# Later weight loads, a ring of queries beside 40 P places, and early gelu products in an attention and gMLP kernel

## The chip, the cores and the metric

The kernel runs on one core of a Trainium2 chip. A core has five engines with queues of their own: TensorE (PE in the profile, with its weight loads as PEld), VectorE (DVE), ScalarE (ACT), GpSimd (POOL) and SyncE (SP), which here only issues DMAs. The metric is device time in microseconds for one execution, as the median of several runs. A profile is one execution of its own, so its time stands beside that median and is not the same number.

## What is computed

Two rounds of an attention layer A and a gated MLP layer B on one sequence of 2048 rows of 512 values, each with a residual addition. A is multi-query attention: 32 heads of 16 values share one key and one value head.

```python
def _A_ref(x, wq, wk, wv, wo):
    ...
    q = (lambda x, *d: x.transpose(*d))((x @ wq).reshape(B, S, H, Dh), 0, 2, 1, 3)
    k = x @ wk
    v = x @ wv
    scores = jnp.einsum('bhqd,bkd->bhqk', q, k) * Dh ** (-0.5)
    p = _softmax(scores, axis=-1)
    o = jnp.einsum('bhqk,bkd->bhqd', p, v)
    return (lambda x, *d: x.transpose(*d))(o, 0, 2, 1, 3).reshape(B, S, H * Dh) @ wo

def _B_ref(x, w_in, w_sp, b_sp, w_out):
    ...
    z = _gelu(jnp.einsum('bsd,df->bsf', x, w_in))
    z1 = z[..., :Fh].copy()
    z2 = _layernorm(z[..., Fh:], axis=-1)
    g = jnp.einsum('ts,bsf->btf', w_sp, z2) + b_sp[None, :, None]
    return jnp.einsum('bsf,fd->bsd', z1 * g, w_out)
x = A_x
x = x + _A_ref(_layernorm(x, axis=-1), A_wq, A_wk, A_wv, A_wo)
x = x + _B_ref(_layernorm(x, axis=-1), B_w_in, B_w_sp, B_b_sp, B_w_out)
```

The last two lines are done twice with the same weights. All values are bfloat16.

## The kernel before

**Scores and P.** A layer has 2048 score blocks of 128 keys by 512 query columns. Up to four blocks are one pack of matmuls (L1262), one block in each of four PSUM banks. Most blocks are turned into P by ScalarE (`do_exp`, L1470), one bank at a time or two neighbouring banks in one instruction. The others go to VectorE as a sum of three clipped linear terms: the first term is read from PSUM (L1384, here a block "on DVE"), the two others are made from it by GpSimd or VectorE, one or two blocks at a time (L1389). A finished P block of 128 x 512 takes one of `NPS` places in the tensor `Pb`; a block on DVE takes three. The product with V (PV, L1525) empties the places again.

**Queries and keys.** `attn_inputs` goes over the 16 tiles of 128 rows: layer norm, a transpose to xnT (the first two tiles by TensorE, the others by a DMA issued on SP, L539), keys and values (L753 to L773), queries (L783, put to `Q` by L793). While not all keys are there, two units run side by side over the keys as they come (the ramp); then the units follow one another. Query rows fall into eight chunks, of 128, 128, 256, 512, 512, 256, 128 and 128 rows.

**The MLP inside the attention.** When a chunk is done it is normalised, multiplied by wo (L942), and its part of layer B begins. `mlp_in` makes one batch for a group of chunks: the products with w_in for z2 (L998, 448 columns at a time) and for z1 (L1044), each ended by a gelu on ScalarE (L1003, L1058). Since exp and gelu need different tables on ScalarE, a batch stops new score packs, loads the gelu table (L1712), runs all its gelus and goes back. There are five batches in a layer: four inside the attention and a last one behind it. The spatial product with w_sp (L1105, `spatial`) is filled in between score packs; its last pass (`last_pass`) runs at the end of a layer: matmuls L1141, the gate product with z1, the product with w_out (L1170) and the addition to X (L1174). In layer 0 the partial sum `gp` is added on TensorE (identity matmul L1139) and the gate product is made by VectorE (L1149). In layer 1 VectorE adds (L1149) and GpSimd multiplies (L1160); `NOID` says which.

**What sets the order.** The order of the instructions on each engine is worked out while the program is built: `Sched` keeps a free time for every engine, every task has an estimated duration, a priority and sometimes a gate (a condition that must hold), and at each step the ready task of the best priority is taken. Smaller numbers come first. On the chip each engine follows this fixed order and waits on semaphores. On PE, packs come first, then PV, then other products that fit before the next pack is due (`pack_due`, `SLACK`); `keep_warm` (L1644) puts in products with zeros where PE would be mostly idle. `SHARE` is the share of blocks for VectorE. SP is one queue too: all loads and all DMA transposes stand in it one behind the other. `setup` puts the loads there:

```python
        for a in range(4, NT, 4):
            loadx(a, a + 4)
        self.ldo = self.dma(self.wo[:], ..., 524288, prio=1)
        self.ldin = self.dma(self.w_in[:], ..., 1835008, prio=1)
        self.ldout = self.dma(self.w_out[:], ..., 917504, prio=1)
```

They are followed there by a load of `bspc`, the bias row of the spatial product, and by the transposes of xn.

Of the kernel before, what the change touches and what calls it, by code (L numbers as in the profile page):

```python
# [12 lines left out]
P = 128  # L13
# [6 lines left out]
S = 2048  # L20
# [272 lines left out]
class Attn:  # L293

    def __init__(self, K, layer):
        self.K = K
        self.layer = layer
        self.kdep, self.vdep, self.qdep = {}, {}, {}
        self.nxt = 0
        self.started = False  # L300
        self.full = False
        self.ugs = []
        for ci, (q0, nq) in enumerate(CHUNKS):
            ng = 512 // nq
# [11 lines left out]
        self.end = None  # L316
        self.chunk_ugs = {}
        for u in self.ugs:
            self.chunk_ugs.setdefault(u.ci, []).append(u)
# [69 lines left out]
class Kernel:  # L389

    SCORE_CAP = 6
    WSP_FROM = 25000
    NPS = 32
    PV_FREE = 6
# [6 lines left out]
    HOLD = 200  # L401
    POOL_ON = 3500
    A_ADJ = 1
    CAP_LINE = 8000
# [7 lines left out]
    NROT = (2, 2)  # L412
    SHARE = 0.31
    SHARE_HI = 0.34
# [8 lines left out]
    RAMP_SHARE1 = 0.0  # L423
    ACT_LOW = 1200
    POOL_MAX = 1400
# [5 lines left out]
    PV_LEAST = 6  # L431
    SLACK = 300
    SLACK_HI = 500
    MISC_T = 1500
    MISC_T2 = 1000
# [5 lines left out]
    def __init__(self, nc, es, ins, out):  # L441
        (self.A_x, self.A_wq, self.A_wk, self.A_wv, self.A_wo, self.B_x, self.B_w_in, self.B_w_sp, self.B_b_sp,
         self.B_w_out) = ins
        self.out = out
        self.nc = nc
        self.es = es
        self.s = Sched(nc)
        self.banks = Pool_(self.s, 8)
        self.score_held = 0
        self.misc_held = 0  # L450
        self.batches = []
        self.batch = None
        self.table = "exp"
# [13 lines left out]
    def alloc(self):  # L467
# [17 lines left out]
        self.w_out = self.sb([P, NF, D], BF16, "w_out")  # L485
        self.Q = self.sb([P, 4, S], BF16, "Q")
        self.xnT2 = self.sb([P, 1, KD, 512], BF16, "xnT2")
# [68 lines left out]
    def job(self, prio, pieces, consumers, tag, kind="misc", batch=None, spare=0, only=None):  # L556
# [4 lines left out]
        def gate():  # L561
            if only is not None and not only():
                return False
            av = self.banks.avail()
            if len(av) < 1 + spare:
                return False
            if kind == "z":
                return self.batch is batch
            if isinstance(kind, int) and self.ai <= kind:
                return False  # L570
            return self.misc_held < self.misc_cap()

        def hook(task):
            b = max(self.banks.avail(), key=lambda b: b.i)
            self.banks.take([b], task)
            hold["b"] = b
            if kind != "z":
                self.misc_held += 1

        last = None  # L580
# [102 lines left out]
    def setup(self):  # L683
# [17 lines left out]
        for a in range(4, NT, 4):  # L701
            loadx(a, a + 4)
        self.ldo = self.dma(self.wo[:], self.A_wo.rearrange("(c p) n -> p c n", p=P), 524288, prio=1)
        self.ldin = self.dma(self.w_in[:], self.B_w_in.rearrange("(kd p) f -> p kd f", p=P), 1835008, prio=1)
        self.ldout = self.dma(self.w_out[:], self.B_w_out.rearrange("(c p) n -> p c n", p=P), 917504, prio=1)
        self.ldv = ldv
# [70 lines left out]

    def queries(self, t, dep, war, prio):
        def qf(e, b, lo, hi):
# [7 lines left out]
        def mk(last, bank):  # L787
            o = self.Q[:, :, t * P:(t + 1) * P]

            def src():  # L790
                return self.ps32[:, bank(), :].rearrange("p (g c) -> p g c", g=4)
            return Task(None, None, None, [last] + list(war), prio - 0.5, tag="qev",
                        alts={"dve": (c_ps(512), lambda e: e.tensor_scalar(o, src(), QSCALE, None, op0=ALU.mult)),  # L793
                              "act": (c_act(512), lambda e: e.activation(o, src(), ACTF.Copy, scale=QSCALE))})
        def later():

            return self.ai < len(self.attns) and self.attns[self.ai].full
        made, outs = self.job(prio, [(lambda e, b: qf(e, b, 0, 2), c_mm(8, 128), [dep, self.ldq]),
# [3 lines left out]
    def attn_inputs(self, layer, xdeps):  # L802
# [5 lines left out]
        for t in range(NT):  # L808
# [8 lines left out]
            A.vdep[t] = [vout]  # L817
            m, q = self.queries(t, ev, war, pr + 0.01 if t < 2 else 4 + 0.05 * t)
            A.qdep[t] = q
# [263 lines left out]
    def spatial(self, B, pi, final):  # L1083
# [5 lines left out]
        for tc in range(4):  # L1089
# [37 lines left out]
    def last_pass(self, B, t, s0, n, sl, lds, zd, final, use):  # L1127

        tc, o = t // 4, (t % 4) * P
        noid = self.NOID[B.layer]  # L1130
        w = n if noid else n + 1
        hs = []
        for f0, f1 in ((0, 4), (4, NF)):
            def gf(e, b, lo, hi, f0=f0):
                ins = None
# [9 lines left out]

            def mk(lp, bank, f0=f0, f1=f1):
                def fn(e):
# [8 lines left out]
            B.all += made  # L1156
            if noid:
                def pf(e, f0=f0, f1=f1):
# [64 lines left out]
    def issue_pack(self, A, blks, deps, bs):  # L1223
        s = self.s
        k = len(blks)

        x = (self.RAMP_SHARE, self.RAMP_SHARE1)[A.layer] if not A.full else self.SHARE if self.pe_line() > self.PE_LINE else self.SHARE_HI
        self.credit = min(self.credit + k * x, self.CREDIT) if x else 0.0
        late = sum(1 for u, kt, j in blks if kt >= self.KT_ACT)
# [28 lines left out]
        def fn(e):  # L1258
            ins = None
            for i, (u, kt, j) in enumerate(blks):  # L1260
                q = self.Q[32 * j:32 * j + 32, u.g0:u.g0 + u.ng, u.q0:u.q0 + u.nq]
                ins = e.matmul(self.ps32[:, jb[i].i, :], self.kT[32 * j:32 * j + 32, u.half, kt * P:(kt + 1) * P], q,  # L1262
                               tile_position=(32 * j, 0), start=True, stop=True)
            return ins
# [515 lines left out]
    def check_batch(self):  # L1780
        if self.batch is None and self.batches:
            b = self.batches[0]
            if all(d.start is not None and d.done <= self.s.t for d in b.pre):
                self.batches.pop(0)
                b.pe_done = False
                self.batch = b
                return True
# [107 lines left out]
```

## Time and profile before

| | |
|---|---|
| median of 3 runs | 1602.91 us (1599.86 to 1607.8) |
| the profiled execution | 1609.46 us, its span 1607.7 us |
| granted TensorE clock over the span | 0.984 of full speed |
| exps (L1470) | 1934 instructions, 1343.4 us busy |
| first terms of blocks on DVE (L1384) | 1278, 835.6 us busy |
| other terms on POOL (L1389) | 1082, 908.7 us busy |
| other terms on DVE (L1389) | 499, 194.1 us busy |
| score matmuls (L1262), PV (L1525) | 4096 and 6652 |
| warm-up products (L1644) | 196 |

A busy time is the time in which an engine had at least one instruction under way; a row's mean is the length of one instruction, and neighbours overlap, so the sum of means can be above the busy time. The number behind a second bar in a row is the idle time of the engine just ahead of these instructions, and behind an arrow stands who ended it. PE's ends are modelled. The granted clock is the share of full speed that TensorE was given. In a timeline a row is a run of like instructions: start, length, engine, line, what it writes and reads, how many.

### The profile page before, as it was taken

The page shows a single profiled execution, that of the slowest core. Times are in us where ns is not written, and L with a number is a line of the kernel's source. Part 1 is how long each engine was busy: PE and PEld are TensorE (multiplying, and loading weights), DVE is VectorE, ACT ScalarE, POOL GpSimd, SP SyncE. Part 2 cuts the span into 40 slices and gives each one's busy share as a digit, 9 for nine tenths or more (in the row PEclk, how much of TensorE's full clock was granted, in tenths as well). Part 3 has the DMA queues.
Part 4 walks back from the last instruction along what each step waited for, and adds up shares of the span by engine and source line. Part 5 has one row for each costly group of instructions (what it writes and reads, how often), then busy time and mean ns, then how long its engine had stood idle before and what let it go on. Part 6 is the DMA issues. An engine that isn't in the chain of part 4 may idle for free.

```text
span 1607.7 us, 36520 instructions
## 1 busy us (share of the span) xinstructions
PE 1499.4 (93%) x14064; PEld 501.0 (31%) x14064; DVE 1389.6 (86%) x2625; ACT 1440.0 (90%) x2107; POOL 1055.5 (66%) x1333
## 2 busy tenths in 40 slices
PE   6999899999999989999988998999999999999998
PEld 3333232222322223223543332322223222322334
DVE  7899978998799997996965999799997899799887
ACT  5999999999899998997379999999998999899950
POOL 5677667776667776875112776677775777667648
PEclk8999999999999999998999999999999999999999
DMA  8000000100001011110120000011010101001111
GB/s 207 18 8 9 1 15 18 33 19 14 14 14 28 14 28 14 22 20 21 40 41 11 8 5 8 8 31 34 15 25 5 27 15 28 14 15 28 28 33 53
DMA packets 123993, 39.73 MB, mean 25 GB/s; under 512 B 116272, under 2 KB 123312, under 8 KB 123824
## 3 DMA queue, kind: packets, MB, share of 16 engines
q1 hardware_dynamic: 123824, 37.41, 10.9%
q8 instruction: 115, 1.88, 0.5%
q14 instruction: 54, 0.44, 0.1%
HBM read 6.98 MB, written 2.10 MB: 6 GB/s over the span
## 4 chain that ended last, share of the span: by engine, by line
ACT 48%; PE 37%; DVE 7%; POOL 3%; issue 3%; DMA 1%; SPq 0%; POOLq 0%; ACTq 0%
ACT Pb L1470 47%; PE ps_all L1525 10%; PE ps_all L1262 10%; PE ps_all L1105 7%; PE ps_all L998 3%; PE ps_all L1044 3%; DVE Pb L1384 3%; POOL z L1160 2%; POOL Pb L1389 1%; DVE Pb L1389 1%; PE ps_all L1170 1%; PE ps_all L942 1%; PE ps_all L783 1%; DMA xnT<-xn 1%; DVE ln_st L624 1%
## 5 line engine op out<-in xcount | busy, mean ns | idle before, releaser
L1470 ACT ACTIVATE Pb<-ps_all 128x512 bf16<-128x512 f32 (+1 forms) x1934 | 1343.4, 867 | 46.0 <-PE ps_all L1262 36.8
L1389 POOL TENSOR_SCALAR Pb<-Pb 128x1024 int16<-128x1024 int16 (+1 forms) x1082 | 908.7, 840 | 359.6 <-DVE Pb L1389 184.9
L1384 DVE TENSOR_SCALAR Pb<-ps_all 128x512 int16<-128x512 f32 x1278 | 835.6, 683 | 100.3 <-PE ps_all L1262 89.0
L1262 PE MATMUL ps_all<-Q,kT 32*128 32x512 bf16 x4096 | 588.3, 389 | 75.0 <-ACT Pb L1470 47.4
L1525 PE MATMUL ps_all<-Pb,V 128*32 128x512 bf16 x6652 | 521.4, 390 | 5.6 <-ACT Pb L1470 1.7
L1262 PEld LDWEIGHTS ps_all<-Q,kT 32*128 32x128 bf16 x4096 | 153.0, 91 | 605.2 <-ACT Pb L1470 370.3
L1105 PE MATMUL ps_all<-wstr,z 128*128 128x512 bf16 x840 | 214.1, 381 | 4.3 <-DMA wstr<-in_B_w_sp_dram 0.8
L1389 DVE TENSOR_SCALAR Pb<-Pb 128x1024 int16<-128x1024 int16 (+1 forms) x499 | 194.1, 419 | 12.7 <-PE ps_all L1525 8.8
L1525 PEld LDWEIGHTS ps_all<-Pb,V 128*32 128x32 bf16 x6652 | 119.2, 95 | 221.4 <-issue 118.1
L1113 DVE TENSOR_TENSOR gp<-ps_all,gp 128x512 f16<-128x512 f32 x168 | 113.6, 687 | 21.1 <-PE ps_all L1105 20.0
L1105 PEld LDWEIGHTS ps_all<-wstr,z 128*128 128x128 bf16 x840 | 67.2, 97 | 105.1 <-DVE Pb L1384 14.9
L615 POOL TENSOR_SCALAR ln_rs<-ln_mv 128x1 f32<-128x1 f32 (+2 forms) x48 | 10.5, 224 | 95.7 <-DVE ln_mv L625 91.1
L1170 PE MATMUL ps_all<-w_out,z 128*128 128x512 bf16 x224 | 58.1, 380 | 2.7 <-POOL z L1160 1.4
L840 DVE CAST oT<-ps_all 128x512 bf16<-128x512 f32 x64 | 43.7, 684 | 15.7 <-PE ps_all L1525 15.4
L998 PE MATMUL ps_all<-w_in,xnT 128*128 128x448 bf16 x256 | 53.1, 367 | 3.9 <-DMA xnT<-xn 3.9
L1044 PE MATMUL ps_all<-xnT,w_in 128*128 128x512 bf16 (+2 forms) x280 | 51.5, 337 | 0.0
L1058 ACT ACTIVATE z<-ps_all 128x512 bf16<-128x512 f32 (+1 forms) x60 | 31.3, 566 | 22.2 <-PE ps_all L1044 22.2
L1011 DVE BATCH_NORM_STATS2 st<-z 128x6 f32<-128x448 bf16 x64 | 36.7, 607 | 15.7 <-ACT z L1003 15.5
L624 DVE BATCH_NORM_STATS2 ln_st<-X 128x6 f32<-128x512 bf16 x64 | 43.2, 681 | 2.7 <-DMA X<-in_A_x_dram 2.6
L1113 DVE TENSOR_TENSOR gp<-ps_all,bspc 128x512 f16<-128x512 f32 x56 | 38.5, 687 | 6.6 <-PE ps_all L1105 5.3
L615 POOL TENSOR_SCALAR rs<-mv 128x4 f32<-128x4 f32 (+2 forms) x10 | 2.3, 233 | 62.3 <-DVE mv L1013 62.3
L1003 ACT ACTIVATE z<-ps_all 128x448 bf16<-128x448 f32 x64 | 30.7, 542 | 13.9 <-PE ps_all L998 13.8
(69 smaller groups left out, 725.9 us busy)
## 6 DMA issues: line engine op xcount, KB each, us to landing
out_dram<-X SPq DMA_DIRECT2D x16, 128.0 KB, 1.7
w_in<-in_B_w_in_dram SPq DMA_DIRECT2D x1, 1792.0 KB, 13.2
X<-in_A_x_dram SPq DMA_DIRECT2D x3, 512.0 KB, 7.4
bspc<-in_B_b_sp_dram SPq DMA_DIRECT2D x8, 128.0 KB, 3.5
w_out<-in_B_w_out_dram SPq DMA_DIRECT2D x1, 896.0 KB, 12.6
wstr<-in_B_w_sp_dram SPq DMA_TRANSPOSE x40, 4.1
X<-in_A_x_dram SPq DMA_DIRECT2D x2, 256.0 KB, 3.3
wq<-in_A_wq_dram SPq DMA_DIRECT2D x1, 512.0 KB, 4.2
```

The costliest lines, as they stand in the source:

```text
L624: a = self.dve(c_ps(512), lambda e, t=t: e.bn_stats(st[:, t, :], X[:, t, :]), [dep], prio, tag="lnst")
L840: ev = Task("dve", c_ps(512), lambda e, u=u, k=k: e.tensor_copy(self.oT[:, k, :], self.ps32[:, u.bank.i, :]), [self.oT_use[k]], 0.2, tag=" ...
L998: ins = e.matmul(self.ps32[:, b, 0:448], self.xnT2[:, buf, kd, o:o + P], self.w_in[:, kd, FH + h * 448:FH + (h + 1) * 448], start=(kd == 0 ...
L1044: ins = e.matmul(self.ps32[:, b, i * nq:(i + 1) * nq], self.w_in[:, kd, f * P:(f + 1) * P], self.xnT2[:, buf, kd, 0:nq], start=(kd == 0), ...
L1105: ins = e.matmul(self.ps32[:, b, :], self.z2[:, (s0 + i) % 8, f * P:(f + 1) * P], self.wstr[:, sl[i // 4][1] + i % 4, :], start=(i == 0), ...
L1113: return Task("dve", c_ps(512), lambda e: e.tensor_tensor(self.gp[:, tc, f, :], self.ps32[:, bank(), :], src, ALU.add), dps, 1.05, tag="gp")
L1170: ins = e.matmul(self.ps32[:, b, :], self.z1[:, tc, f, o:o + P], self.w_out[:, f, :], start=(f == 0), stop=(f == NF - 1))
L1262: ins = e.matmul(self.ps32[:, jb[i].i, :], self.kT[32 * j:32 * j + 32, u.half, kt * P:(kt + 1) * P], q, tile_position=(32 * j, 0), start=T ...
L1384: return lambda e: e.tensor_scalar(self.Pi[:, dst():dst() + k, :], self.ps32[:, bank:bank + k, :], EBIAS + lo, lo, op0=ALU.add, op1=ALU.max)
L1389: return lambda e: e.tensor_scalar(self.Pi[:, dst():dst() + k, :], self.Pi[:, src():src() + k, :], lo, 1.0, op0=ALU.add, op1=ALU.mult)
L1470: return e.activation(self.Pb[:, s0:s0 + n, :], self.ps32[:, b0:b0 + n, :], ACTF.Exp, scale=ESCALE)
L1525: ins = e.matmul(self.ps32[32 * j:32 * j + 32, u.bank.i, :], self.V[:, var, kt, :], self.Pb[:, sl.i, :], tile_position=(0, 32 * j), start= ...
```

## The change

The loads of wo, w_in and w_out get a gate (planned time above 45 us) and a later priority; the load of the bias row gets the gate that the slabs of w_sp have. `Q` holds eight tiles instead of sixteen, and a later tile may be written when the last block of the tile eight before it has been issued; its priority becomes better than that of spatial products. The 8 KB per partition go to eight more P places. The z products of the next batch may start before the batch is opened, up to two of them; the batch opens when they have started. In layer 1 the second half of every fourth tile in the last pass takes layer 0's way. Four constants of the plan change (SHARE, ACT_LOW, SLACK, MISC_T).

```diff
-    NPS = 32
+    W_FROM = 45000
+    NPS = 40
+    QT = 8
...
+    Z_EARLY = 2
+    RAMP_DVE = 0
+    RAMP_LINE = 8000
+    NOID_T = (0, 1, 2)
...
-    SHARE = 0.31
+    SHARE = 0.32
...
-    ACT_LOW = 1200
+    ACT_LOW = 1300
...
-    SLACK = 300
+    SLACK = 280
...
-    MISC_T = 1500
+    MISC_T = 1300
...
-        self.Q = self.sb([P, 4, S], BF16, "Q")
+        self.Q = self.sb([P, 4, self.QT * P], BF16, "Q")
...
             if kind == "z":
-                return self.batch is batch
+                return self.batch is batch or self.early is batch and self.early_n < self.Z_EARLY
...
-        self.ldo = self.dma(self.wo[:], self.A_wo.rearrange("(c p) n -> p c n", p=P), 524288, prio=1)
-        self.ldin = self.dma(self.w_in[:], self.B_w_in.rearrange("(kd p) f -> p kd f", p=P), 1835008, prio=1)
-        self.ldout = self.dma(self.w_out[:], self.B_w_out.rearrange("(c p) n -> p c n", p=P), 917504, prio=1)
+        def late():
+
+            return s.t > self.W_FROM
+        self.ldo = self.dma(self.wo[:], self.A_wo.rearrange("(c p) n -> p c n", p=P), 524288, prio=2.5, gate=late)
+        self.ldin = self.dma(self.w_in[:], self.B_w_in.rearrange("(kd p) f -> p kd f", p=P), 1835008, prio=2.5, gate=late)
+        self.ldout = self.dma(self.w_out[:], self.B_w_out.rearrange("(c p) n -> p c n", p=P), 917504, prio=2.5, gate=late)
...
-            o = self.Q[:, :, t * P:(t + 1) * P]
+            o = self.Q[:, :, t % self.QT * P:(t % self.QT + 1) * P]
...
-            return self.ai < len(self.attns) and self.attns[self.ai].full
+            if self.ai >= len(self.attns) or not self.attns[self.ai].full:
+                return False
+            return t < self.QT or A.nxt >= A.last_block[t - self.QT]
...
-            m, q = self.queries(t, ev, war, pr + 0.01 if t < 2 else 4 + 0.05 * t)
+            m, q = self.queries(A, t, ev, war, pr + 0.01 if t < 2 else 4 + 0.05 * t if t < self.QT else 3 + 0.02 * t)
...
                     lb = self.dma(self.bspc[:], self.B_b_sp[tc * 512:(tc + 1) * 512].partition_broadcast(P), 131072,
-                                  self.bs_use, prio=2, tag="ldb")
+                                  self.bs_use, prio=2, tag="ldb", gate=lambda: self.s.t > self.WSP_FROM)
...
-        noid = self.NOID[B.layer]
-        w = n if noid else n + 1
         hs = []
         for f0, f1 in ((0, 4), (4, NF)):
-            def gf(e, b, lo, hi, f0=f0):
+
+            add = self.NOID[B.layer] and (f0 == 0 or t % 4 in self.NOID_T)
+            w = n if add else n + 1
+
+            def gf(e, b, lo, hi, f0=f0, noid=add):
...
-                q = self.Q[32 * j:32 * j + 32, u.g0:u.g0 + u.ng, u.q0:u.q0 + u.nq]
+                o = u.q0 % (self.QT * P)
+                q = self.Q[32 * j:32 * j + 32, u.g0:u.g0 + u.ng, o:o + u.nq]
...
             if all(d.start is not None and d.done <= self.s.t for d in b.pre):
+
+                if b.fin is None and self.Z_EARLY and self.early is not b:
+                    self.early, self.early_n = b, 0
+                    return True
+                if self.early is b and self.early_n < self.Z_EARLY and self.attn_on():
+                    return False
+                self.early = None
                 self.batches.pop(0)
```

`RAMP_DVE` guards a further rule for the share in the ramp of layer 1; at 0 that rule is off.

More of the change, by code (lines that the diff above doesn't have):

```diff
@@ L316, in __init__ @@
         self.end = None
+        self.last_block = {}
+        for i, (u, kt, j) in enumerate(self.blocks):
+            for t in range(u.q0 // P, (u.q0 + u.nq) // P):
+                self.last_block[t] = i + 1
         self.chunk_ugs = {}
@@ L452, in __init__ @@
         self.batch = None
+        self.early = None
+        self.early_n = 0
         self.table = "exp"
@@ L578, in hook @@
                 self.misc_held += 1
+            elif self.early is not None:
+                self.early_n += 1
         last = None
@@ L776, in keys, with queries @@
         return made, outs[0], outs[1]
-    def queries(self, t, dep, war, prio):
+    def queries(self, A, t, dep, war, prio):
         def qf(e, b, lo, hi):
@@ L1144, in last_pass, with mk @@
             m = f0 + 2
-            def mk(lp, bank, f0=f0, f1=f1):
+            def mk(lp, bank, f0=f0, f1=f1, noid=add):
                 def fn(e):
@@ L1156, in last_pass @@
             B.all += made
-            if noid:
+            if add:
                 def pf(e, f0=f0, f1=f1):
@@ L1227, in issue_pack @@
         x = (self.RAMP_SHARE, self.RAMP_SHARE1)[A.layer] if not A.full else self.SHARE if self.pe_line() > self.PE_LINE else self.SHARE_HI
+        if not A.full and A.layer and self.RAMP_DVE and self.dve_backlog() < self.RAMP_DVE and self.pe_line() < self.RAMP_LINE:
+            x = self.RAMP_SHARE
         self.credit = min(self.credit + k * x, self.CREDIT) if x else 0.0
@@ L1783, in check_batch @@
             if all(d.start is not None and d.done <= self.s.t for d in b.pre):
+                if b.fin is None and self.Z_EARLY and self.early is not b:
[3 more added lines that the diff above has]
+                    return False
+                self.early = None
                 self.batches.pop(0)
```

## The prediction

> **What bounds the kernel now.** I read the page's busy line and its chain first, then busy time by stage, then the costliest groups with shapes kept apart, and last the timelines of three places: the start, one gelu batch, the end.
>
> ```profile
> PE 1499.4 (93%) x14064; PEld 501.0 (31%) x14064; DVE 1389.6 (86%) x2625; ACT 1440.0 (90%) x2107; POOL 1055.5 (66%) x1333
> ...
> ACT 48%; PE 37%; DVE 7%; POOL 3%; issue 3%; DMA 1%; SPq 0%; POOLq 0%; ACTq 0%
> ```
>
> PE has the higher share, but its ends are modelled, so the stages must decide. In the answer by stage (stretch, its length, then busy us of PE, PEld, DVE, ACT, POOL, then the granted clock) look at the fourth busy number:
>
> ```profile
> 0.00:40.00 40.00, 27.35 (x265) 13.95 (x265) 28.45 (x81) 21.17 (x26) 22.35 (x62) 0.80 0.82 207
> ...
> 240.20:417.30 177.10, 165.83 (x1572) 47.38 (x1569) 162.67 (x298) 174.84 (x254) 126.82 (x158) 0.98 0.10 22
> 417.30:433.40 16.10, 14.96 (x95) 6.68 (x96) 7.46 (x18) 10.62 (x19) 7.77 (x11) 1.00 0.00 0
> ...
> 793.20:1024.20 231.00, 206.80 (x2236) 75.97 (x2235) 188.74 (x380) 216.84 (x310) 121.89 (x152) 1.00 0.08 16
> ...
> 1547.20:1607.70 60.50, 54.67 (x367) 27.31 (x366) 48.45 (x87) 5.51 (x9) 34.82 (x39) 1.00 0.20 57
> ```
>
> In a score stage such as 240 to 417 ScalarE (ACT) is idle for 2.3 us of 177.1: **it is the bound**. Of the span's 1607.7 - 1440.0 = 167.7 us of idle ACT, 18.8 lie in the first 40 us; 31.6 in the eight gelu batches inside the attentions (5.5 in the one shown, 2.6 to 5.9 in all), where PE is the busy engine; 29.1 in the turn between the layers (756.8 to 793.2); 14.2 in the score stage after it; 55.0 in the end; the rest, some 19, is spread thinly over the other score stages. So the change can win in three ways: fewer or cheaper exps, less idle ACT at the start and in the batches, a shorter end.
>
> **The exps.** The instruction order of the changed kernel has 920 exps of two banks (884 before) and 970 of one (1050), that is 8 blocks fewer on ACT; VectorE (DVE) takes them (1286 instead of 1278).
>
> ```profile
> L1470 ACT ACTIVATE Pb<-ps_all 128x1024 bf16<-128x1024 f32 x884 | 894.6, 1100 | 30.1 <-PE ps_all L1262 25.9 <-PE ps_all L1525 1.5
> ...
> L1470 ACT ACTIVATE Pb<-ps_all 128x512 bf16<-128x512 f32 x1050 | 598.4, 671 | 15.9 <-PE ps_all L1262 10.9 <-PE ps_all L1525 3.7
> ```
>
> These durations overlap: 884 x 1.100 + 1050 x 0.671 = 1677 us, while the page has 1343.4 busy for both together, so one hides 333.6/1934 = 0.172 of the next. A pair costs ACT 0.928 us, a single 0.499. The change: 80 x 0.499 - 36 x 0.928 = **-6.5 us**. Taken at face value the durations would give 14, too much. The 8 blocks put 8 x 0.68 on DVE and two products each on POOL or DVE, both with slack in score stages (162.67 and 126.82 of 177.1). Ends -8 and -4. More pairs is what eight more places can buy; waits for a place are already small: 5.3 us of ACT on the PV product (L1525). With SHARE, SLACK, ACT_LOW and MISC_T they all alter the plan of score stages; no row prices that: from -5 to +8 on their thin idle of 19 us, I take -1.
>
> **The start.** Later loads and bspc move this part of SP's queue:
>
> ```profile
> 5.75 2.98 SPq L530 DMA_DIRECT2D w_in<-in_B_w_in_dram  x1
> 8.77 1.32 SPq L530 DMA_DIRECT2D w_out<-in_B_w_out_dram  x1
> 10.12 4.05 SPq L530 DMA_DIRECT2D bspc<-in_B_b_sp_dram  x1
> 14.22 13.95 SPq L539 DMA_TRANSPOSE z<-xn  x7
> ...
> 26.67 1.02 ACT L1470 ACTIVATE Pb<-ps_all 128x1024 bf16<-128x1024 f32 x1 [5.73 <-PE ps_all L1262]
> ```
>
> The third tile's xn is ready at about 8.5 us, but its transpose is issued at 14.22, behind 8.9 us of other issues (0.51 for wo before those shown), and its key product runs only at 25.09, behind 3.3 MB still in flight; ACT stands 5.73 us at 20.94. In the new order ten transposes follow the X loads directly, about 2 us each (13.95/7), and ACT uses up a tile in 8 x 0.46 = 3.7 us (fewer with DVE's share): the hole goes, and most of the 0.81 after it. What is late next is DVE: it worked off 7 us of layer norm statistics in that hole, which must now fit between key evacuations. From 27 to 45 ACT has another 3.2 us of short gaps in front of PE. Best -9.8, worst 0 (DVE as late as the DMA was); I take **-6**. The moved loads cost nothing: wo is first used at 110.2 us, w_in at 225.2, and a load of this size landed 13.2 us after its issue. On SP they now stand before the last transposes of the ramp: 4.05 us of bspc in front of the twelfth tile and 0.51 of wo in front of the last; such a tile is needed some 30 us after the third, against 20 us of issuing, so this is covered; if not, 4 us at most.
>
> Two rules of the Trainium skill speak against this part. "DMA: Bandwidth & Descriptors", Rules for kernel authors, wants a DMA issued early and waited on late. By the rule the load gives up cover and gains nothing: 0; by the rows the cover is over 50 us either way and the issue itself is what blocks: -6. I follow the rows. "TensorE: Matmul & The Clock Gate", Why this matters for your kernels, warns that an idle PE falls to half clock, and the plan's warm-up products fall from 196 to 96 (68 to 16 before the first batch). The rows: clock 0.66 over 27 to 47, where a score pack takes 0.61 instead of 0.39. The 3.2 us of gaps belong to about 13.7 us of half clock; if the whole ramp from 13.5 to 45 ran so, 7.4 of gaps would leave -2.4. But 40 of the warm products filled the very hole that goes, so I keep -6.
>
> **Gelu products early.** In the new order five of the eight batches have one z2 product (4 matmuls) ahead of the batch, between score packs; the other three still begin with the whole run.
>
> ```profile
> 417.30 1.28 ACT L1712 ACT_TABLE_LOAD   x1
> 418.44 6.23 PE L998 MATMUL ps_all<-w_in,xnT 128*128 128x448 bf16 x32 [2.04 <-DMA xnT<-xn]
> ...
> 419.79 0.98 ACT L1003 ACTIVATE z<-ps_all 128x448 bf16<-128x448 f32 x2 [0.99 <-PE ps_all L998]
> ```
>
> A batch is PE's pace: 6.2 us of z2 and about 6 of z1. One product taken out is 4 x 6.23/32 = 0.78 us, and in those five a PV of 8 (0.55) no longer stands between the last z1 products: 5 x 1.33 = 6.7. PE also waits for the transposed xnT (7.1 us in all, 2.04 here); moved ahead, that wait meets ACT while it has up to six banks of scores (6 x 0.46 = 2.8 us) to work off. But the PE time is taken from score packs, behind a waiting product stand all later packs, and a bank is held: I take **-5**, ends -10 and +3.
>
> **The Q ring** moves queries 8 to 15 behind the first batch (64 of 256 matmuls). Their ring slots are old by then (tile 8 needs only chunk 0 done), so nothing waits: 0.
>
> **The end.** In layer 1 four of POOL's 32 gate products become a PE addition and a DVE product.
>
> ```profile
> 1571.38 31.80 POOL L1160 TENSOR_TENSOR z<-gp,z 128x512 bf16<-128x512 f16 x32 [2.35 <-DVE gp L1149]
> ```
>
> ```profile
> L1160 POOL TENSOR_TENSOR z<-gp,z 128x384 bf16<-128x384 f16 x16 | 14.9, 934 | 0.0
> ```
>
> POOL runs without a break to the end of the kernel, so 4 x 0.934 = -3.7. Against it: 18 more spatial matmuls (L1105) are left after the last score, 12 of them ahead of the first last-pass product. At 0.216 each (24 in 5.18 on the chain), 12 cost +2.6, with 8 more PV (0.55) and less the 0.56 that PE stood for z2n: +2.6. And PE becomes the next limit: 112 last-pass matmuls, 12 additions, 6 spatial and 112 of OUT are 7.3 + 0.7 + 1.3 + 24.2 = 33.5 us, plus about 1 before the first OUT and 2.7 for the last addition and store: 37.2 against 37.9 now, so of 3.7 only 0.7 arrives. Together +1.9; I take **+1.5**, ends -2.5 and +4.
>
> **Sum.** -6.5 - 1 - 6 - 5 + 1.5 = **-17 us**. The profiled execution took 1609.5 (span 1607.7 and 1.8 around it), giving 1592.5. It is 6.6 above the median of the three runs, 1602.9, so the forecast for a median is **1586**.
>
> **Rivals.** (a) *The room is given back*, chance 0.14: DVE keeps the start as late as before (no -6), and the early products take from the packs what they give (no -5): 1602.9 - 6 = 1597; with the end at +4 1599. For it: DVE is 86% busy and the batches are PE's pace. Against: the hole at 20.94 ended on a key tile, not on DVE. (b) *New waits in the score stages*, slower, chance 0.11: the order on each engine is fixed by estimated durations, and five early products with their 2 us DMA waits, 64 moved query products and a new share bring PE late to packs when ACT is empty. The score stage from 793 shows the price, 14.2 us of ACT idle in gaps of about 0.5. The forecast's 17 us are used up by 34 such gaps, +0.5% takes 50; were the other seven large stages to show 4 us more each, it would be 1602.9 - 17 + 28 = 1614. Against: idle ACT there is 1 to 3%, and packs still go first. (c) *More than I count*, 0.05: every part at its good end, 1602.9 - 32 = 1571. (d) That the 40 places or the early products do nothing lies in (a): three batches are in fact unchanged.
>
> **Chances.** Forecast 0.70, its own range 1575 to 1597. Adding the nearer part of (a) and of (b) up to 1604 and a little of (c) down to 1574 holds about 8 in 10. Measurements of this kernel tell 0.5% (8 us) from no change: faster 0.75, same 0.14, slower 0.11.
>
> **What would show it.** Right: no gap near 5 us of ACT in the first 40 us and its busy time there near 27; exps busy near 1337; idle ACT in the eight batches near 26; the POOL run at the end near 28, PE packed beside it, the stretch from the last exp to the end no shorter than 59. Wrong: gaps of 0.3 us or more before exps all over the score stages, a kernel whose start still waits (on DVE instead of a tile), or xnT waits on PE in front of score packs.

## The result and the profile after

The changed kernel takes **1581.1 us** in the median (1579.77 to 1585.25), the kernel before 1603.1 us in the runs beside it (1599.86 to 1607.8). The ratio is 0.9865 with an interval of 0.9834 to 0.9896: 22 us or 1.35% faster, where 17 us were forecast and 1586 us given. The profiled execution took 1579.77 us, the shortest of the four measured; its span is 1577.7 us.

The page's busy line and its chain of work, by engine:

```profile
PE 1487.2 (94%) x13992; PEld 499.3 (32%) x13992; DVE 1385.1 (88%) x2627; ACT 1430.6 (91%) x2063; POOL 1043.5 (66%) x1269
...
ACT 54%; PE 33%; DVE 8%; issue 3%; DMA 2%; POOL 0%; SPq 0%; ACTq 0%
```

ScalarE works 9.4 us less and its idle time falls from 167.7 us to 1577.7 - 1430.6 = 147.1: a third of the gain is less work on it, two thirds are idle time that went. POOL has left the chain. By stage (stretch, its length, busy us of PE, PEld, DVE, ACT and POOL, granted clock):

```profile
0.00:40.00 40.00, 28.73 (x265) 13.69 (x266) 29.04 (x85) 26.42 (x32) 20.19 (x58) 0.80 0.65 133
...
234.20:420.20 186.00, 178.27 (x1729) 53.90 (x1727) 171.28 (x310) 183.27 (x259) 139.04 (x162) 1.00 0.10 21
420.20:433.10 12.90, 12.19 (x74) 5.33 (x73) 7.21 (x19) 10.33 (x21) 6.40 (x8) 1.00 0.00 0
773.70:1007.90 234.20, 212.02 (x2208) 75.42 (x2207) 194.58 (x390) 220.20 (x315) 120.91 (x152) 0.99 0.09 16
1516.50:1577.70 61.20, 58.19 (x398) 30.42 (x390) 51.75 (x92) 5.56 (x10) 29.95 (x32) 1.00 0.25 63
```

Row by row: 5.25 us more ACT work done by 40 us (21.17 before); a score stage that still leaves ACT idle for 2.7 us; the second gelu batch over 3 us shorter (1.4 us against the second profile of the kernel before, e1, below); the stage after the turn with 14.0 us of idle ACT (14.2 before), unchanged; the end 0.6 us longer (the rows are cut to tenths).

The exps with their shapes kept apart, 920 pairs and 970 singles as planned; as one group they are busy for 1336.3 us (1343.4 before):

```profile
L1494 ACT ACTIVATE Pb<-ps_all 128x1024 bf16<-128x1024 f32 x920 | 939.1, 1105 | 25.8 <-PE ps_all L1286 22.4 <-PE ps_all L1549 0.8
...
L1494 ACT ACTIVATE Pb<-ps_all 128x512 bf16<-128x512 f32 x970 | 568.4, 689 | 11.8 <-PE ps_all L1286 11.1
```

The start in the timeline (start, length, engine, line, what, how many, idle before): the transposes now follow the X loads, and nine pairs run without a gap where a hole of 5.73 us stood:

```profile
3.96 1.27 SPq L542 DMA_DIRECT2D X<-in_A_x_dram  x2
8.93 22.07 SPq L551 DMA_TRANSPOSE z<-xn  x10
13.48 8.43 ACT L1494 ACTIVATE Pb<-ps_all 128x1024 bf16<-128x1024 f32 x9 [1.37 <-PE ps_all L1286]
22.45 1.02 ACT L1494 ACTIVATE Pb<-ps_all 128x1024 bf16<-128x1024 f32 x1 [0.53 <-PE ps_all L1286]
```

The second batch: z2 products start 0.9 us ahead of the table load, and seven gelus follow it at once (before, only two, after a wait of 0.99 us):

```profile
419.36 5.09 PE L1017 MATMUL ps_all<-w_in,xnT 128*128 128x448 bf16 x26
420.24 1.28 ACT L1736 ACT_TABLE_LOAD   x1
421.53 0.20 ACT L1736 ACTIVATE dummy<-dummy 128x1 f32<-128x1 f32 x1
421.64 3.13 ACT L1022 ACTIVATE z<-ps_all 128x448 bf16<-128x448 f32 x7
```

**Where the time went**, from the ScalarE rows of five profiles. "e1" is the first experiment below; it runs the instructions of the kernel before in the same order on every engine but SP, so it is in effect a second profile of that kernel, and a quicker one. What the two disagree on is scatter between executions. The last two columns are the neighbours used further below. All in us:

| | before | e1 | after | e5 | e8 |
|---|---|---|---|---|---|
| span | 1607.7 | 1600.1 | 1577.7 | 1589.4 | 1593.0 |
| up to the first exp | 13.5 | 13.6 | 13.5 | 12.9 | 12.9 |
| exps, busy | 1343.4 | 1342.4 | 1336.3 | 1337.3 | 1339.5 |
| ACT idle between exps, ramp of layer 0 | 13.6 | 13.0 | 7.5 | 18.4 | 14.8 |
| the same, first stage of layer 1 | 14.2 | 14.1 | 14.0 | 13.1 | 14.0 |
| the same, all other score stages | 13.8 | 11.9 | 11.6 | 12.8 | 18.6 |
| eight gelu batches, length | 112.3 | 107.3 | 97.4 | 97.6 | 94.4 |
| turn between the layers | 36.4 | 36.3 | 36.2 | 36.2 | 36.8 |
| last exp to the end | 60.6 | 61.4 | 61.2 | 61.1 | 62.0 |

A batch is counted from the end of the last exp ahead of it to the start of the first one behind it, and the rows of a column add up to its span. (The recorded expectations count slightly otherwise: 112.1 for the batches before, 98.1 after.) Against e1 the span loses 22.4 us, as the medians do: batches 9.9, exps 6.1, the first ramp 5.5, the rest 0.9. The ramp's row is the one that a single execution shows least reliably; more profiles of it stand under "The start" below.

### The profile page after: what moved, and what is told of

Its sections match the earlier page's. It is cut to its first block, busy times and chain, and to the rows that moved or that the text cites. A ratio compares the mean times of both kernels' runs of the same rounds, so it can differ in the third digit from the quotient of the medians.

```text
span 1577.7 us, 36212 instructions
## 1 busy us (share of the span) xinstructions
PE 1487.2 (94%) x13992; PEld 499.3 (32%) x13992; DVE 1385.1 (88%) x2627; ACT 1430.6 (91%) x2063; POOL 1043.5 (66%) x1269
## 4 chain that ended last, share of the span: by engine, by line
ACT 54%; PE 33%; DVE 8%; issue 3%; DMA 2%; POOL 0%; SPq 0%; ACTq 0%
ACT Pb L1494 53%; PE ps_all L1549 8%; PE ps_all L1286 8%; PE ps_all L1124 5%; DVE Pb L1408 3%; PE ps_all L1063 3%; PE ps_all L1017 3%; PE ps_all L1191 2%; DMA z<-xn 1%; PE ps_all L961 1%; DVE Pb L1413 1%; DVE ln_st L638 1%; DVE gp L1132 1%; PE ps_all L800 1%; ACT L1736 1%
## 5 line engine op out<-in xcount | busy, mean ns | idle before, releaser
L1494 ACT ACTIVATE Pb<-ps_all 128x1024 bf16<-128x1024 f32 (+1 forms) x1890 | 1336.3, 892 | 37.6 <-PE ps_all L1286 33.5
L1413 DVE TENSOR_SCALAR Pb<-Pb 128x1024 int16<-128x1024 int16 (+1 forms) x493 | 190.1, 418 | 8.7 <-PE ps_all L1549 6.9
L859 DVE CAST oT<-ps_all 128x512 bf16<-128x512 f32 x64 | 43.7, 684 | 13.8 <-PE ps_all L1549 13.4
L1030 DVE BATCH_NORM_STATS2 st<-z 128x6 f32<-128x448 bf16 x64 | 35.8, 602 | 13.7 <-ACT z L1022 13.6
L800 PE MATMUL ps_all<-z,wq 128*128 128x128 bf16 x512 | 41.0, 225 | 0.6 <-DVE Pb L1408 0.2
```

The source lines that it names most:

```text
L800: ins = e.matmul(self.ps32[:, b, g * P:(g + 1) * P], self.wq[:, kd, g * P:(g + 1) * P], self.xnT(t, kd), start=(kd == 0), stop=(kd == KD - 1))
L1413: return lambda e: e.tensor_scalar(self.Pi[:, dst():dst() + k, :], self.Pi[:, src():src() + k, :], lo, 1.0, op0=ALU.add, op1=ALU.mult)
L1494: return e.activation(self.Pb[:, s0:s0 + n, :], self.ps32[:, b0:b0 + n, :], ACTF.Exp, scale=ESCALE)
```

## The experiments

All run beside the kernel before, whose medians there were 1602.6 to 1604.6 us. Ratios are to that kernel.

### 1. The queue alone: e1_spq

In the kernel before, the four issues (wo, w_in, w_out and the first bias row) are taken out of SP's finished queue and put behind the ramp's transposes. No other engine's order changes.

```diff
+        sp = K.s.prog["sp"]
+        late = [x for x in sp[:12] if x[3] in (K.ldo, K.ldin, K.ldout) or x[3].tag == "ldb"]
+        rest = [x for x in sp if all(x is not y for y in late)]
+        n = max(i for i, x in enumerate(rest[:30]) if x[3].tag == "TA") + 1
...
+        K.s.prog["sp"] = rest[:n] + late + rest[n:]
```

> The kernel before with one thing moved: the issues of wo, w_in, w_out and the first bias row stand in SP's queue behind the 14 transposes of the first ramp; the order on every other engine is the same as before. Theory (the first transposes wait behind these loads, and nothing else at the start matters): the gap of 5.7 us of ScalarE at 20.9 us goes, idle time between the first exp and 226 us falls from 13.6 us by about 6, and the time falls by 6 us (0.4%). Rival 1 (the gain of the start is the new order of all engines): the gap stays over 3 us and the time falls by under 2 us. Rival 2 (VectorE is late at once): the gap closes but returns as several of 0.5 to 1 us, and the time falls by under 3 us.

1603.29 us, ratio 0.9996 [0.9971, 1.002]: nothing, as Rival 1 had it. The timeline says why:

```profile
9.16 18.72 SPq L539 DMA_TRANSPOSE z<-xn  x7
...
21.12 0.62 PE L1525 MATMUL ps_all<-Pb,V 128*32 128x512 bf16 x4 [0.36 <-ACT Pb L1470]
21.52 3.35 PE L1644 MATMUL ps_all<-wq,zero 128*32 128x512 bf16 x40
24.80 0.40 PE L753 MATMUL ps_all<-z,wk 128*128 128x128 bf16 x4
...
26.38 1.02 ACT L1470 ACTIVATE Pb<-ps_all 128x1024 bf16<-128x1024 f32 x1 [5.32 <-PE ps_all L1262]
```

The first of these transposes is issued at 9.16 us instead of 14.22, yet ACT's hole is still 5.32 us. The third tile's key product at 24.80 waits for no DMA any more; it stands behind PV and 40 warm-up products, in the order that was planned with the loads ahead of the tile. The kernel before has the same rows, and its key product waits for no DMA either: by the trace's landing records its tile was there at 22.3 us, but the warm-up products ran until its start at 25.09.

```profile
21.39 3.77 PE L1644 MATMUL ps_all<-wq,zero 128*32 128x512 bf16 x40
25.09 0.40 PE L753 MATMUL ps_all<-z,wk 128*128 128x128 bf16 x4
```

**Freeing the queue alone gains nothing.** The warm-up products that stood in the hole as filler were what held the key product in the end.

### 2. The old queue under the new order: e5_spq_back

The reverse, in the changed kernel: the four issues go back behind the X loads, all other engines keep the new order. (`NDMA`, the number of semaphores that DMAs take in turn, is raised so that the moved loads can have theirs.)

```diff
-    NDMA = 24
+    NDMA = 40
...
+        early = [x for x in sp if x[3] in (K.ldo, K.ldin, K.ldout)] + [first]
+        rest = [x for x in sp if all(x is not y for y in early)]
+        K.s.prog["sp"] = rest[:8] + early + rest[8:]
```

> The changed kernel with one thing moved: wo, w_in, w_out and the first bias row are issued right behind the X loads again, ahead of all transposes; the order on every other engine is that of the changed kernel. Theory (the free SP queue is needed as well as the new order: keys of the third tile can't come before its transpose): a gap of ScalarE of 5 to 10 us appears between 14 and 30 us, PE waits for the transposes of xn instead of 2.9 us for over 6, and the time is 5 to 10 us above the changed kernel. Rival (the order of PE and VectorE alone made the start shorter; the queue is not in the way on the chip): the start keeps under 3 us of new gaps and the time is within 2 us of the changed kernel.

1591.13 us, ratio 0.9918 [0.9891, 0.9946]: 10 us behind the changed kernel, as the theory had it.

```profile
9.47 4.00 SPq L542 DMA_DIRECT2D bspc<-in_B_b_sp_dram  x1
...
13.52 23.48 SPq L551 DMA_TRANSPOSE z<-xn  x9
21.72 0.59 PE L770 MATMUL ps_all<-z,wk 128*128 128x128 bf16 x4 [8.34 <-DMA z<-xn]
22.98 1.94 ACT L1494 ACTIVATE Pb<-ps_all 128x1024 bf16<-128x1024 f32 x2 [8.17 <-PE ps_all L1286]
```

Now it is the transpose that PE waits for, 8.34 us, and ACT with it; the ramp's idle time is 18.4 us instead of 7.5, nearly all of the 11.7 us between the two spans. So the start's gain needs both: the free queue, and the order on PE that the planner makes when it knows of the free queue. Neither e1 nor e5 was planned anew, so no accident of planning is in these two.

### 3. Early products taken away, and alone: e3_noearly, e4_early_alone

In the changed kernel no product starts ahead of its batch:

```diff
-    Z_EARLY = 2
+    Z_EARLY = 0
```

> The changed kernel without early gelu products (Z_EARLY 0), planned anew. Theory (early products shorten the batches): the eight gelu batches inside the attentions take 108 to 113 us together (98.1 in the changed kernel, 112.1 before) and the time is 10 to 14 us above the changed kernel. Rival (the batches became shorter because the xnT transposes and the clock fell better in this plan): the batches stay under 103 us and the time is within 5 us of the changed kernel.

In the kernel before, only the early products are added:

```diff
+    Z_EARLY = 2
...
-                return self.batch is batch
+                return self.batch is batch or self.early is batch and self.early_n < self.Z_EARLY
...
+                if b.fin is None and self.Z_EARLY and self.early is not b:
+                    self.early, self.early_n = b, 0
+                    return True
+                if self.early is b and self.early_n < self.Z_EARLY and self.attn_on():
+                    return False
+                self.early = None
```

> The kernel before with early gelu products alone, planned anew; only three of the eight batches have one product ahead of the run in this plan. Theory (each batch with an early product is about 2 us shorter): the eight batches take 104 to 108 us together and the time falls by 4 to 8 us. Rival (the product only takes from the score packs what it gives to the batch): the batches are shorter, but idle ScalarE in the score stages grows by as much, and the time stays within 3 us of before.

Without them 1594.05 us, 0.9935 [0.9913, 0.9958], 13 us behind the changed kernel, as the theory had it: the batches are 106.2 us long instead of 97.4, and another 5.3 us are idle ACT between exps. (3.4 of these lie in the first ramp, where the order of e3 is that of the changed kernel; they are scatter, see "The start".) Alone 1606.51 us, 1.0017 [1.0, 1.0033]: no gain, as the rival had it. There the batches do shorten, to 100.2 from e1's 107.3, but the idle time between exps grows by 5.6 us, the turn by 2.6 and the end by 2.6. Waits for score packs are not the reason, at 35.1 us in all against 36.7 in e1. 3.0 of the 5.6 are waits for a place in P that PV has yet to empty (engine, what it wants to write, whom it waits for: us in all, times, longest; e1 first, then e4), and the rest is in small pieces:

```profile
ACT Pb L1470 <- PE ps_all L1525: 3.0, 10, 0.6
```

```profile
ACT Pb L1475 <- PE ps_all L1530: 6.0, 12, 1.1
```

### 4. The room taken away, and alone: e8_32_places, e7_room_alone

In the changed kernel 32 places for P as before (the ring of queries stays); and in the kernel before, the ring and 40 places without anything else.

```diff
-    NPS = 40
+    NPS = 32
```

> The changed kernel with 32 places (the ring of queries kept), planned anew; all eight batches have an early product in this plan, pairs fall to 891. Theory (early products and the start carry the gain, places little): exps +2 to +4 us, the time 2 to 6 us above the changed kernel. Rival (early products pay only where P has room, as their trial alone suggests): score stages and ends take back what the batches gain, and the time is 8 to 15 us above the changed kernel.

```diff
-    NPS = 32
+    NPS = 40
+    QT = 8
...
+            return t < self.QT or A.nxt >= A.last_block[t - self.QT]
...
+                o = u.q0 % (self.QT * P)
+                q = self.Q[32 * j:32 * j + 32, u.g0:u.g0 + u.ng, o:o + u.nq]
```

> The kernel before with the ring of queries and 40 places alone, planned anew (921 pairs and 979 single exps in its order). Theory (the places buy pairs and little else): exps about as busy as before (by the durations 1343), batches 107 to 113, time within 4 us of before. Rival (the places loosen the whole order): idle ScalarE in the score stages falls by 3 us or more and the time by 5 to 10 us.

With 32 places 1596.4 us, 0.9947 [0.9928, 0.9966], 15 us behind the changed kernel, as the rival had it. The batches are even shorter (94.4 us), since in this plan all eight have early products, but the table shows 14.3 us more idle ACT between exps. The waits for a place in this kernel and, in the second fence, in the changed one:

```profile
ACT Pb L1494 <- PE ps_all L1549: 6.2, 9, 1.3
```

```profile
ACT Pb L1494 <- PE ps_all L1549: 0.8, 1, 0.8
```

With 32 places ACT waits 6.2 us in all for places; with 40 this is one wait of 0.8 us. (Before it was 5.3 us in 15 waits, in e1 3.0.) Waits for score packs grow as well, from 33.5 to 39.1 us in all. The room alone is worth nothing: 1602.07 us, 0.9993 [0.997, 1.0015]. In the plans tried, **early products and places pay only together**. That the products spend just what the places provide fits the waits for places in e4 and e8, but these are 3 and 5 us of larger losses, so it is not shown that they are the whole reason.

### 5. The end: e2_end

In the changed kernel no gate product of layer 1 leaves POOL's way:

```diff
-    NOID_T = (0, 1, 2)
+    NOID_T = (0, 1, 2, 3)
```

> The changed kernel with the last pass of layer 1 as before (all 32 gate products on GpSimd, no additions by identity matmuls there); the order up to that pass is that of the changed kernel. Theory (the four products taken from GpSimd are worth their 3.7 us, of which PE takes back some): GpSimd's run at the end is 31.8 instead of 28.3 us, and the end after the last exp is 61.2 + 1 to 3.5 us. Rival (PE is the bound of the end in any case): the end is within 0.5 us of 61.2.

1583.21 us, 0.9861 [0.9834, 0.9888]: 2.1 us behind the changed kernel, with intervals that overlap, so the time alone does not decide. The profiles do, as the theory had it: from the last exp to the end it takes 63.0 us instead of 61.2 (61.1 in e5, which has the changed order there too). POOL's last run here, and then in the changed kernel with the last run of PE beside it:

```profile
1547.54 31.79 POOL L1181 TENSOR_TENSOR z<-gp,z 128x512 bf16<-128x512 f16 x32 [7.53 <-DVE gp L1170]
```

```profile
1543.20 28.34 POOL L1181 TENSOR_TENSOR z<-gp,z 128x512 bf16<-128x512 f16 x28 [7.52 <-DVE gp L1170]
...
1566.29 8.58 PE L1191 MATMUL ps_all<-w_out,z 128*128 128x512 bf16 x39
```

Four products less shorten POOL's run by 3.45 us and the end by 1.9: POOL stops at 1571.54, but PE goes on with 39 products of w_out without a pause until 1574.87, and the kernel ends 6.2 us after POOL instead of 4.5 before.

### 6. How much of it is the plan: e6_ctrl, e9_ctrl_275, e10_before_295, e11_const_back

The order is planned anew for every edit, so a small edit may move much. Four controls change planner constants alone. `SLACK` says by how many ns another product on PE may run past the planned time of the next pack. The changed kernel has 280, the kernel before 300:

```diff
-    SLACK = 280
+    SLACK = 285
```

> The changed kernel with SLACK 285 instead of 280, planned anew: nothing that matters is altered, so this shows how much a plan of the same kind differs by accident. Theory (the parts carry the gain): within 5 us of the changed kernel, batches 95 to 102 us together. Rival (the changed kernel's plan is a lucky one of many): 6 to 15 us above it, by longer ends, turns and score stages, with early products in the batches all the same.

```diff
-    SLACK = 280
+    SLACK = 275
```

> The changed kernel with SLACK 275 instead of 280, planned anew: a second neighbour of its plan, on the other side of 280. If the parts carry all of the gain, its time is within 5 us of the changed kernel (1576 to 1587). If the plan with 280 is a lucky one, as the neighbour with 285 suggests (11 us above it), it is again 6 to 15 us above, with the batches (98) and exps (1337) as short as in the changed kernel and the loss in ramps, turn and end.

In the kernel before, `SLACK = 295` instead of 300:

> The kernel before with SLACK 295 instead of 300, planned anew: a neighbour of its plan. If the plan of before is itself chosen among its neighbours, the time is 5 to 12 us above before, and then the parts together are worth more than neighbours of the changed kernel show against before. If it is an ordinary plan, the time is within 4 us of before.

In the changed kernel, the four constants of the kernel before:

```diff
-    SHARE = 0.32
+    SHARE = 0.31
-    ACT_LOW = 1300
+    ACT_LOW = 1200
-    SLACK = 280
+    SLACK = 300
-    MISC_T = 1300
+    MISC_T = 1500
```

> The changed kernel with the four constants of the plan as before (SHARE 0.31, ACT_LOW 1200, SLACK 300, MISC_T 1500), planned anew; 12 blocks fewer on VectorE. Theory (the constants only pick a plan; loads, places and early products carry the gain): exps about 1343 us busy, batches 96 to 102, the time 4 to 12 us above the changed kernel, like its neighbours. Rival (the new parts need these constants): nothing is left of the gain, 1598 or more.

| | median us | ratio | exps busy | batches | ACT idle between exps |
|---|---|---|---|---|---|
| changed kernel | 1581.1 | 0.9865 [0.9834, 0.9896] | 1336.3 | 97.4 | 33.1 |
| SLACK 275 | 1579.76 | 0.9855 [0.9841, 0.987] | 1336.7 | 96.7 | 35.8 |
| SLACK 285 | 1592.4 | 0.9917 [0.9888, 0.9945] | 1337.1 | 97.5 | 39.5 |
| old constants | 1589.91 | 0.9925 [0.9908, 0.9941] | 1342.7 | 95.4 | 37.3 |
| before, SLACK 295 | 1604.4 | 1.0011 [0.9995, 1.0027] | 1342.7 | 110.3 | 40.8 |

Going from 280 to 285 costs 11 us, as the rival had it; going to 275 costs nothing. With 285 exps and batches are as in the changed kernel. The profile has 6.4 us more idle time between exps, 3.8 of it in the first stage of layer 1; another 2.4 lie in the first ramp, where both kernels have the same order, and are scatter. (The profiled execution of SLACK 285 was its shortest, 1587.4 us, so its row shows only part of the 11.) The plan of the kernel before is an ordinary one: its neighbour is within 2 us of it. This bounds what the other experiments can say: the 13 us of e3 and the 15 of e8 hold up to about 11 us of such scatter each, and the single losses must not be added. e1 and e5 keep their plan, and e2 keeps it up to the last pass; these carry none of it.

The four plans with the loads, places, early products and last pass of the change average 1585.8 us, 17 under the kernel before; the other 5 us of the 22 come with the plan that SLACK 280 or 275 happens to give. The old constants bring the exps back to 1342.7 us. That plan leaves 12 blocks more to ScalarE (2822 instead of 2810) and has 927 pairs; e7 has 921 pairs and 1343.5 us. So the 6.5 us go with the constants, which hand blocks to VectorE; the pairs that more places buy do not lower the exps by themselves.

### 7. A try for more: e12_cap5

The ramp may have scores in five banks instead of four:

```diff
-        return self.SCORE_CAP if self.attns[self.ai].full else 4
+        return self.SCORE_CAP if self.attns[self.ai].full else 5
```

> A try for a faster kernel: the changed kernel with five score banks instead of four in the two ramps, planned anew. If ScalarE's gaps of 0.5 us before packs in the ramp of layer 1 come from too few score banks, its idle time there falls from 14.0 us to under 8 and, with an ordinary plan elsewhere, the time is 1580 to 1590. If the banks are needed by keys, queries and PV in the ramp, the idle time stays over 12 us and the time is 1588 to 1600.

1590.08 us, 0.992 [0.9906, 0.9935]. The first stage of layer 1 has 17.0 us of idle ACT instead of 14.0, so in this plan a fifth bank does not help it. The other score stages have 22.3 us instead of 11.6, most of the growth in waits for P places, of which one alone is 7.1 us:

```profile
ACT Pb L1494 <- PE ps_all L1549: 11.2, 8, 7.1
```

No run here beats the changed kernel; SLACK 275 lies 1.3 us under it, within the spread.

## Why the prediction was right, step by step

**The bound.** ScalarE was the bound of the score stages and still is: in the one shown it is idle for 2.7 us of 186.

**The exps**, -6.5: 1343.4 to 1336.3 us on the page, -7.1. The step that took the overlap of 0.172 us off every exp was right; face value, 14 us, would have been wrong by twice. Its source is the constants (e11). The places do buy pairs, 921 in e7 where the kernel before has 884, but with these alone the exps stay at 1343.5 us.

**Score stages**, -1: other idle time 13.8 to 11.6 us, or -0.2 against e1. Rightly small for this plan. It is also the term with the widest neighbours: +7.0 us in e8, +10.7 in e12.

**The start**, -6: idle time in the first ramp 13.6 to 7.5 us (-5.5 against e1), 26.42 us of ACT work in the first 40 where near 27 was named. The reason was only half right: I held the issues in SP's queue to be the cause and the 40 warm-up products to be filler; the key product at 25.09 stood behind these, and no longer behind "3.3 MB still in flight". e1 shows that the fixed order of PE held the keys as well, e5 that the queue is needed too. The weighing against the Trainium skill's rule on early issues ("DMA: Bandwidth & Descriptors", Rules for kernel authors) held in the changed kernel (e5: 10 us lost when the big loads go ahead of the transposes), with the addition that only the re-planned order collects it. DVE, named as the next to be late, held PE's keys and scores for at most 1.3 us at a time between 12 and 40 us.

The size was in part luck of the profiled execution. Up to the first batch, e2, e3 and e6 run the order of the changed kernel, and e1, e4 and e10 that of the kernel before (e1 but for SP, e4 but for the last 4 us), so there are four profiles of each start:

| up to the first batch, us | ACT idle between exps | time at half clock |
|---|---|---|
| before, e1, e4, e10 | 13.6, 13.0, 13.6, 13.2 | 20.5, 20.5, 23.9, 20.5 |
| after, e2, e3, e6 | 7.5, 10.9, 10.9, 9.9 | 27.3, 37.5, 37.5, 34.1 |

The means are 13.3 and 9.8: the start is worth about 3.5 us, from 2 to 6 with the execution.

**The clock.** The same stretch of the changed kernel and, in the second fence, of e2, which has the same order there (the fourth busy number is ACT's, the clock stands behind POOL's):

```profile
13.50:60.00 46.50, 41.00 (x374) 14.19 (x376) 38.79 (x98) 40.90 (x53) 24.33 (x43) 0.74 0.49 106
```

```profile
13.50:60.00 46.50, 40.83 (x346) 14.31 (x342) 35.27 (x91) 37.09 (x46) 20.71 (x37) 0.63 0.40 76
```

ACT gets 3.8 us less done in e2. (The granted clock is either full or half in these traces; the times at half clock come from its records.) From 30 to 60 us e2 has half clock up to 52.1, the changed kernel only from 37.5 to 47.7, and ACT is idle for 6.2 against 3.7 us. Another 1.0 us comes before, where PE in e2 waits 1.25 us for a transpose.

The warning of the Trainium skill that an idle PE falls to half clock ("TensorE: Matmul & The Clock Gate", Why this matters for your kernels) spoke against losing 100 warm-up products, and the prediction set its price: with the whole ramp at half clock, -2.4 of the -6 would be left. In e2 the half clock lasts from 18.0 to 52.1 us, and 2.1 us are left against e1. So setting that price aside was the weak step of this part. The page names gaps of over about 3 us as the trigger; in e2 the longest gap of PE between 10 and 55 us is 1.25 us, so it does not explain this half clock. Over the whole span nothing of it shows: 51.2 us at half clock before, 27.3 in e1, 30.7 after. Whether the missing warm-up products are the cause is not shown, since no run changes them alone. e12, with 68 of them ahead of the first batch as before (the changed kernel has 16), has only 13.7 us of half clock there and 5.9 us of idle ACT; but e8 has 72, 37.5 us and 14.8.

**Gelu batches**, -5: the **term that was mis-sized** most. They shortened by 14.9 us between the two profiles, of which 5.0 are scatter between the two profiles of the old order; 9.9 stay, and e2 and e5, with the same order in the batches, agree (97.6 us both); idle ACT in them is 19.0 us where near 26 was named. Three errors: in the five batches that have an early product it was worth 1.7 us each, 8.6 in all, instead of 1.33; the other three shortened too, by 1.3 together; and I took a discount for packs that come late which this plan does not pay. A discount of that size is real elsewhere: e4 and e8 pay it in full, partly as waits for places. The prediction priced the 40 places only through pairs of exps; that they spared the discount here is likely, not shown. The xnT waits that I set against the gain (7.1 us of PE and PEld before, 4.1 in e1) have gone; e2 has one of 0.7 us.

**The ring of queries**, 0: no wait on it appears.

**The end**, +1.5: 60.6 to 61.2 us, +0.6 (-0.2 against e1). POOL's run 31.80 to 28.34 us, its start 26.7 us after the last exp instead of 24.2 (+2.5, where +2.6 was worked out), PE the next limit: all three as forecast.

**The sum and the rivals.** -7.1 - 2.2 - 6.0 - 14.9 + 0.6 and -0.4 elsewhere make the 30.0 us between the two spans; 7.6 of these are scatter between two profiles of the old order, and the medians differ by 22. The forecast of 17 fell short by what the batches gave, 4.9 us more than their term; in executions whose start gives only 2 to 4 us the two errors partly cancel, so the sum is nearer than its terms. That the four plans average just 17 us may well be chance. Rivals (a), room given back, and (b), new waits in the score stages, did not come true in the changed kernel; what they describe of early products and score stages happens in its neighbours, in e4 and in e8.

**What stays open:** how the 17 us divide among the parts, since each edit that is planned anew carries up to 11 us of scatter; what lowers the clock in the ramp of the changed kernel; and which decision of the planner makes SLACK 285 so much worse than 280.

## What to carry to other kernels

Where a static order is worked out from estimates, moving a DMA pays only if the order on the other engines is made again with it: test the queue and the order apart, each with the other held fixed. A part that frees a resource and a part that spends it must be tried together; here places alone and early products alone gave nothing, in one plan each. And before a few microseconds are put down to a part, run two or three neighbouring plans to see how far the time moves by itself, and profile the same order more than once: one and the same start left ScalarE idle for 7.5 to 10.9 us, with 27 to 38 us at half clock up to the first batch.

## What was not expected of the hardware

The length of an issue is not a price of the instruction. In the changed kernel the same loads took SP:

```profile
34.23 0.58 SPq L542 DMA_DIRECT2D bspc<-in_B_b_sp_dram  x1
...
54.35 0.58 SPq L542 DMA_DIRECT2D w_in<-in_B_w_in_dram  x1
```

Before, with the X loads and other weights just issued, they took 4.05 and 2.98 us; in e1 w_in took 0.51 at 43.56 us and bspc, right behind w_in and w_out, 2.52. The long issues are those with megabytes issued just ahead and still moving, so the 8.9 us that I counted as a fixed cost were mostly a wait for these. The rows show this as a pattern; no run takes it apart further.

Two profiles with the same order on every engine but SP (before and e1) differ by 7.6 us of span, 5.0 of them in the batches, with 51.2 and 27.3 us at half clock. A part of a few microseconds is better judged against two profiles of the kernel before than against one.
